# An attention block beside a gated MLP on one core: a third VectorE buffer, q masks and head packing by few DMAs over DRAM, the last softmax sums on TensorE, and new DMA times in the schedule model

## The chip, the core and the metric

The kernel runs on one core of a Trainium2 chip (trn2). A time is device microseconds of one execution. Each comparison below was run in rounds on one chip, the kernel beside the kernel before, and ratios are computed from these rounds: the mean time of one kernel's fast runs over the mean of the other's fast runs of the same rounds, so a ratio is not quite that of the medians that I quote. An interval is the 95% interval of that ratio. Profiles are of single executions, and single executions of one program differ here by about 1%.

## The reference

```python
xn = layernorm(x)                         # x: 1 x 2048 x 512, bf16
qkv = xn @ wqkv                           # H = 32 heads of Dh = 16
scores = einsum("bhqd,bhkd->bhqk", q, k) * 16 ** -0.5
o = einsum("bhqk,bhkd->bhqd", softmax(scores), v)
gate, up = xn @ W_gate, xn @ W_up         # 512 -> 1792
return x + o @ wo + (relu(gate) * up) @ W_down
```

32 heads times 2048 x 2048 scores are 134 million exponentials. They are the bulk of the work outside TensorE.

## The kernel before

ScalarE takes about 80% of the exponentials from PSUM (659 instructions on 1024 or 1536 columns). VectorE makes the other 20% (100 groups of four tiles) from bit arithmetic in five steps per group. TensorE makes the scores, the weighted sums of v ("PV"), the projections and the MLP, which are slotted in between. A score matmul sums over 32 rows, which hold two heads of 16, so q must be masked: `qm[:, slot, ee]` holds the rows of every second head and zeros elsewhere. ScalarE writes its exponentials into a ring of NRING buffers ("slots"), VectorE writes its own into NDR buffers; PV reads both, and a slot or buffer can be written again only when PV has read it.

The order of all instructions on all engines is fixed when the kernel is built. A small list scheduler in the kernel places each operation by an assumed duration and latency; on the chip every engine then executes its list in order, with semaphores. If an operation takes longer than the scheduler believed, whatever was placed behind it waits. The parts that the change touches:

```python
NRING = 7; PV_LAG = 7.0; PV_MIN = 0; NDR = 2     # NDR: VectorE's buffers
D_GROUPS = 100; D_SKIP = 10; D_TAIL = 12; D_LEAD = 11.0; D_WAIT = 6.0
RIDE = 40.0

def dma(fn, kb, ...):                            # the scheduler's idea of a DMA
    return G.op("SP", 120 + 3 * kb, fn, ..., lat=1900 + 2 * kb, ...)

def proj_q(c4, gg, ...):                         # q tile -> masked q
    G.op("DVE", 610, lambda e: e.tensor_copy(qT[:, tr.slot, :], bank_of(t, sub)), ...)
    for ee in range(2):
        for j in range(4):
            r0 = 32 * j + DH * ee
            dma(lambda e: e.dma_start(qm[r0:r0 + DH, tq.slot, ee, :], qT[r0:r0 + DH, tr.slot, :]), 16, ...)

def normalise(c4, gg, ee):                       # divide by the softmax sums
    G.op("DVE", 610, lambda e: e.tensor_copy(o_sb[...], ps_b[:, 0, :]), ...)
    dma(... rsum[:, par, :], o_sb[DH:128:32, to.slot, :] ..., 8)       # gather the sums
    G.op("DVE", 260, lambda e: e.reciprocal(rrec[...], rsum[...]), prio=-940)
    dma(... rec_scr[n] <- rrec ..., 8)                                 # to DRAM
    dma(... rb[...] <- rec_scr[n] broadcast to 32 rows each ..., 256)  # and back, spread
    G.op("POOL", 1200, lambda e: e.tensor_tensor(oT_of(tn), o_sb[...], rb[...], ALU.mult), ...)
    # [cut] the second of a pair of heads is packed beside the first by four DMAs of 16 KB
```

The softmax here doesn't subtract the row's maximum and nothing guards it: scores larger than these inputs give would overflow.

Of the kernel before, what the change touches and what calls it, by code (L numbers as in the profile page):

```python
# [5 lines left out]
BF16 = mybir.dt.bfloat16  # L6
# [22 lines left out]
NRING = 7  # L29
PV_LAG = 7.0  # L30
PV_MIN = 0
NWS = 3
NQ = 3
NDR = 2
KD = (1, 5, 9, 13)
D_GROUPS = 100
D_SKIP = 10
D_TAIL = 12
D_LEAD = 11.0
D_WAIT = 6.0  # L40
# [20 lines left out]
class Tile:  # L61
    def __init__(self, name="", pool=None, allowed=None):
        self.name = name
        self.pool = pool
        self.allowed = allowed
        self.slot = None
        self.w = []
        self.r = []


class Op:
    __slots__ = ("eng", "dur", "fn", "deps", "order", "prio", "acq", "name", "idx", "start", "end",
                 "done", "left", "users", "signal", "sem", "val", "waits", "stream", "lat", "seq", "hb", "after", "mode", "rows", "opens")


class Graph:
# [6 lines left out]
    RIDE = 40.0  # L83
# [11 lines left out]
    def op(self, eng, dur, fn, reads=(), writes=(), prio=0.0, order=(), name="", stream=None, lat=None, after=None, mode=None, rows=()):  # L95
        o = Op()
        o.rows = frozenset(rows)
        o.opens = None
        o.mode = mode
        o.eng, o.dur, o.fn, o.prio, o.name = eng, dur, fn, prio, name  # L100
        o.lat = self.LAT[eng] if lat is None else lat
        o.stream = stream
        o.after = after
        o.deps = {}
        o.order = set(order)
        o.acq = []
        o.done = False
        o.idx = len(self.ops)
        for t in reads:
            for w in t.w:  # L110
                o.deps[w] = True
        for t in writes:
            if t.pool is not None and not t.w:
                o.acq.append(t)
            for w in t.w:
                if w.eng == eng and eng == "PE":
                    o.order.add(w)
                else:
                    o.deps[w] = True
            for r in t.r:  # L120
                if r.eng == eng and eng in ("PE", "ACT"):
                    o.order.add(r)
                else:
                    o.deps[r] = True
        for t in reads:
            t.r.append(o)
        for t in writes:
            t.w.append(o)
        o.deps.pop(o, None)
        o.order.discard(o)  # L130
        self.ops.append(o)
        return o

    def run(self):
# [49 lines left out]
        def place(at, e, o):  # L184
            for t in o.acq:
                if t.slot is not None:
                    continue
                i = slot_for(t)[1]
                c = t.pool.cur[i]
                if c is not None:  # L190
                    for u in c.w + c.r:
                        if u.eng == e and e in ("PE", "ACT"):
                            o.order.add(u)
                        else:
                            o.deps[u] = True
                t.slot = i
                t.pool.cur[i] = t
            o.start = at
            o.end = at + o.dur + o.lat
            o.done = True  # L200
            o.seq = len(self.queue[e])
            self.queue[e].append(o)
            free[e] = max(free[e], at + o.dur)
            if o in cand[e]:
                cand[e].remove(o)
            for u in o.users:
                u.left -= 1
                if u.left == 0:
                    cand[u.eng].append(u)
# [12 lines left out]
        def blanks(at, o):  # L222

            while self.open is not None:
# [5 lines left out]
                b = self.op("PE", self.BLANK, self.fill, mode="col", name="blank")  # L230
                b.users, b.left = [], 0
                b.order.update(self.open)
# [5 lines left out]
        self.nblank = 0  # L238
        total = len(ops)
        while n < total:  # L240
# [27 lines left out]
            if e == "PE" and o.opens is not None:  # L268
                self.open = o.opens or None
            n += 1  # L270
# [117 lines left out]
def bass_parallel_sum__mha_block__glu_gated_reglu__prompt_kernel(  # L388
# [12 lines left out]
    rec_scr = nc.dram_tensor("rec_scr", [32, 4, 512], FP32, kind="Internal")  # L401

    with ExitStack() as es:
# [25 lines left out]
        qT = sb("qT", [128, 2, 512], BF16)  # L429
# [10 lines left out]
        oT2 = sb("oT2", [128, 2, 512], BF16)  # L440
        zeros = sb("zeros", [128, 512], BF16)
# [10 lines left out]
        P_qr = Pool("qr", 2)  # L452
# [5 lines left out]
        P_oT = Pool("oT", 10)  # L458
# [23 lines left out]
        t_qz = [Tile() for _ in range(NQ)]  # L482
        for i in range(1, NQ):
            G.op("POOL", 1000, lambda e, i=i: e.memset(qm[:, i, :, :], 0.0), writes=[t_qz[i]], prio=-480)
# [6 lines left out]
        def dma(fn, kb, writes=(), reads=(), prio=0.0, stream=None, order=(), name="dma", after=None):  # L491
            return G.op("SP", 120 + 3 * kb, fn, reads=reads, writes=writes, prio=prio, stream=stream or ("o", len(G.ops)),
                        lat=1900 + 2 * kb, order=order, name=name, after=after)

        x_src = x2.rearrange("(m p) d -> p m d", p=128)
        t_x = [Tile("x", P_x) for _ in range(NB)]
# [110 lines left out]
        def bank_of(t, sub=0):  # L607
            return ps_sc[:, 3 * t.slot + sub, :] if t.pool is P_sc else ps_b[:, t.slot, :]
# [13 lines left out]

        def proj_q(c4, gg, prio=0.0, tile=None, sub=0, eng="DVE", slots=None):
# [5 lines left out]
            if eng == "ACT":  # L629
# [3 lines left out]
                         reads=[t, t_mask], writes=[t_q1], prio=prio - 0.5)  # L633
                o.deps[tq.w[0]] = True
                tq.r.append(o)
            else:
                tr = Tile("qr", P_qr)
                G.op("DVE", 610, lambda e: e.tensor_copy(qT[:, tr.slot, :], bank_of(t, sub)), reads=[t], writes=[tr], prio=prio)
                for ee in range(2):
                    for j in range(4):  # L640
                        r0 = 32 * j + DH * ee
                        dma(lambda e, ee=ee, r0=r0: e.dma_start(qm[r0:r0 + DH, tq.slot, ee, :], qT[r0:r0 + DH, tr.slot, :]), 16,  # L642
                            reads=[tr] + t_qz, writes=[tq], prio=prio - 60, stream=("q%d" % (4 * ee + j), (4 * c4 + gg) % 2))
                        o = G.ops[-1]
                        for w in tq.w[:-1]:
                            o.deps.pop(w, None)
                            o.order.discard(w)
                        if (ee or j) and tq in o.acq:
                            o.acq.remove(tq)
# [80 lines left out]
        def heat(e):  # L730
            ins = None
            for _ in range(14):
                ins = e.matmul(ps_b[:, 1, :], zeros[:, 0:128], zeros[:], start=True, stop=True)
            return ins
        G.op("PE", 6000, heat, reads=[t_zero], writes=[tw0], prio=-900)
# [139 lines left out]
        pv_tile, last_rec, where = {}, {}, {}  # L875

        def normalise(c4, gg, ee):
# [5 lines left out]
            pr = upos(c4, gg, ee, NT) + 1  # L883
            ts, trr, tsc, trb = Tile("rs"), Tile("rr"), Tile("sc"), Tile("rb", P_rb)
            par = n % 2
            if n >= 2:
                ts.r.extend(last_rec[n - 2][0].r)
                trr.r.extend(last_rec[n - 2][1].r)
            dma(lambda e: e.dma_start(rsum[:, par, :], o_sb[DH:128:32, to.slot, :]), 8, reads=[to], writes=[ts], prio=pr - 50, stream=("n1", n % 4))
            G.op("DVE", 260, lambda e: e.reciprocal(rrec[:, par, :], rsum[:, par, :]), reads=[ts], writes=[trr], prio=-940)  # L890
            dma(lambda e: e.dma_start(rec_scr[n].rearrange("j (i q) -> (j i) q", q=16), rrec[:, par, :]), 8,
                reads=[trr], writes=[tsc], prio=pr - 50, stream=("n2", n % 4))
            last_rec[n] = (ts, trr)
            dma(lambda e: e.dma_start(rb[:, trb.slot, :], rec_scr[n].unsqueeze(1).to_broadcast([4, 32, 512])), 256,
                reads=[tsc], writes=[trb], prio=pr - 50, stream=("n3", n % 4))
            tn = Tile("oT", P_oT)
            G.op("POOL", 1200, lambda e: e.tensor_tensor(oT_of(tn), o_sb[:, to.slot, :], rb[:, trb.slot, :], ALU.mult),  # L897
                 reads=[to, trb], writes=[tn], prio=pr)
            if (c4, gg) == (NB - 1, NGG - 1):
                t_oT[(c4, NGG + ee)] = tn  # L900
            elif ee == 0:
                t_oT[(c4, gg)] = tn
            else:
                tw = t_oT[(c4, gg)]
                first_w = list(tw.w)
                for j in range(4):
                    dma(lambda e, j=j: e.dma_start(oT_of(tw)[32 * j + DH:32 * j + 32, :], oT_of(tn)[32 * j:32 * j + DH, :]), 16,
                        reads=[tn], writes=[tw], prio=pr, stream=("c%d" % j, gg % 2))
                    o = G.ops[-1]
                    for w in tw.w[:-1]:  # L910
                        if w not in first_w:
                            o.deps.pop(w, None)
                            o.order.discard(w)

        def pv_group(key, kt, u):
# [12 lines left out]
            for k in range(3 if on else 1):  # L928
# [9 lines left out]
                if first and k == 0:  # L938
                    G.ops[-1].opens = [G.ops[-1]]
                if last and k == (2 if on else 0):  # L940
                    G.ops[-1].opens = []
# [89 lines left out]
        tz = Tile("fin", P_sc, [0])  # L1031
        tz2 = Tile("fin2", P_b, [1])
        for i in range(4):
            out_rows(3, i, [5], False, True, pr=NU + 10 + i, tile=tz if i < 3 else tz2, sub=i if i < 3 else 0)

        def blank(e):
            ins = None
            for j in range(4):
                ins = e.matmul(ps_b[32 * j:32 * j + VN, 0, :], zeros[:, 0:VN], zeros[:], start=False, stop=False, tile_position=(0, 32 * j))  # L1039
            return ins  # L1040
        G.fill = blank
# [30 lines left out]
```

## Time and profile before

| | |
|---|---|
| time, median (of its 4 runs in the rounds of the comparison) | 890.1 us |
| the profiled execution | 898.1 us, span 896.3 us |
| first exponential starts / last ends | 17.6 / 876.4 us |
| ScalarE idle between the two | 101 us |
| TensorE's gaps over 1 us between the two | 9, together 20.9 us |

The prediction shows the lines of this profile and how each is read. Two more, which the argument needs later, come from the view of waits (engine and line that waited, what ended the wait; us in total, times, longest):

```profile
ACT ring L1020 <- PE ps_b L933: 54.8, 40, 5.9
...
DVE rrec L890 <- DMA rsum<-Wv: 10.1, 6, 2.8
```

The first says that ScalarE, before 40 of its exponentials, sat idle until TensorE was through with a PV matmul (L933). It was not waiting for scores. In one of these waits (timeline):

```profile
417.65 0.39 PE L952 MATMUL ps_sc<-qm,kT 32*128 32x512 bf16 x3
...
419.49 0.61 PE L933 MATMUL ps_b<-ring,v_aug 128*17 128x512 bf16 x8
...
419.93 1.45 ACT L1020 ACTIVATE ring<-ps_sc 128x1536 bf16<-128x1536 f32 x1 [2.00 <-PE ps_b L933]
```

The three scores of that exponential were done at 418.04, and it started only at 419.93, on the PV of 419.49 (whose end the profile models). Matching every exponential with its scores in the trace gives 38 waits, 54.0 us together, before which the scores had been ready for 1.67 us (median). In kernel.py an exponential depends on a PV only through the ring slot that it writes, so this row is ScalarE waiting for a free slot.

The second row is VectorE held by the small DMA that gathers the softmax sums. Each row names the last event before the wait ended, so by itself it is a pointer and not a proof.

### The profile page before, as it was taken

The page shows a single profiled execution, that of the slowest core. Times are in us where ns is not written, and L with a number is a line of the kernel's source. Part 1 is how long each engine was busy: PE and PEld are TensorE (multiplying, and loading weights), DVE is VectorE, ACT ScalarE, POOL GpSimd, SP SyncE. Part 2 cuts the span into 40 slices and gives each one's busy share as a digit, 9 for nine tenths or more (in the row PEclk, how much of TensorE's full clock was granted, in tenths as well). Part 3 has the DMA queues.
Part 4 walks back from the last instruction along what each step waited for, and adds up shares of the span by engine and source line. Part 5 has one row for each costly group of instructions (what it writes and reads, how often), then busy time and mean ns, then how long its engine had stood idle before and what let it go on. Part 6 is the DMA issues. An engine that isn't in the chain of part 4 may idle for free.

```text
span 896.3 us, 22022 instructions
## 1 busy us (share of the span) xinstructions
PE 823.7 (92%) x9722; PEld 239.2 (27%) x9722; DVE 774.7 (86%) x1116; ACT 762.2 (85%) x666; POOL 58.3 (7%) x58
## 2 busy tenths in 40 slices
PE   7999999999989989999989999999899999998992
PEld 3322222222222222222223222222222322222320
DVE  7999999899968979998896999998797989997842
ACT  4899989898969989899777999998797989985770
POOL 4100000100000000000000000000000000000000
PEclk8999999999999999999999999999899989998996
DMA  5023112111011111122010121112000121121001
GB/s 170 20 72 92 45 31 52 31 34 33 8 34 31 48 48 38 27 52 55 20 28 20 43 61 28 46 49 58 26 19 23 37 58 37 46 73 37 23 20 36
DMA packets 90031, 38.32 MB, mean 43 GB/s; under 512 B 72848, under 2 KB 85840, under 8 KB 89936
## 3 DMA queue, kind: packets, MB, share of 16 engines
q1 hardware_dynamic: 89936, 36.92, 15.8%
q8 instruction: 76, 1.25, 0.6%
q14 instruction: 19, 0.16, 0.1%
HBM read 31.33 MB, written 2.36 MB: 38 GB/s over the span
## 4 chain that ended last, share of the span: by engine, by line
PE 42%; DVE 38%; ACT 9%; DMA 5%; SPq 4%; issue 2%; POOLq 0%; POOL 0%
PE ps_b L617 15%; DVE dring L968 12%; PE ps_sc L952 10%; ACT ring L1020 9%; PE ps_b L933 9%; DVE dring L984 7%; DVE dring L985 5%; PE ps_b L952 4%; DVE dring L980 4%; SPq L642 3%; DVE dring L982 3%; PE ps_b L1039 3%; DVE up_sb L779 2%; DVE hT L783 2%; DVE Wv L882 1%
## 5 line engine op out<-in xcount | busy, mean ns | idle before, releaser
L1020 ACT ACTIVATE ring<-ps_sc 128x1536 bf16<-128x1536 f32 (+1 forms) x659 | 757.7, 1260 | 103.8 <-PE ps_b L933 54.8
L968 DVE TENSOR_SCALAR dring<-ps_b 128x512 uint16<-128x512 f32 x400 | 273.8, 685 | 40.5 <-PE ps_b L952 33.6
L952 PE MATMUL ps_sc<-qm,kT 32*128 32x512 bf16 x1648 | 267.3, 390 | 12.0 <-ACT ring L1020 5.0
L952 PE MATMUL ps_b<-qm,kT 32*128 32x512 bf16 x400 | 155.4, 388 | 15.5 <-DVE dring L968 13.4
L933 PE MATMUL ps_b<-ring,v_aug 128*17 128x512 bf16 x1648 | 141.0, 385 | 4.2 <-DVE Wv L882 4.2
L985 DVE TENSOR_TENSOR dring<-dring 128x2048 bf16<-128x2048 bf16 x100 | 126.6, 1266 | 0.2
L984 DVE TENSOR_TENSOR dring<-dring 128x2048 f16<-128x2048 bf16 x100 | 123.9, 1239 | 0.0
L952 PEld LDWEIGHTS ps_sc<-qm,kT 32*128 32x128 bf16 x1648 | 62.9, 91 | 227.0 <-ACT ring L1020 180.0
L1039 PE MATMUL ps_b<-zeros 128*17 128x512 bf16 x1020 | 84.0, 391 | 0.0
L897 POOL TENSOR_TENSOR x_sb<-Wv,rb 128x512 bf16<-128x512 f32 x26 | 37.9, 1458 | 665.0 <-DMA rb<-rec_scr 551.5
L617 PE MATMUL ps_b<-Wd,hT 128*32 128x512 bf16 x896 | 69.6, 403 | 7.5 <-DMA x_sb<-x_sb 7.5
L980 DVE TENSOR_SCALAR dring<-dring 128x2048 uint16<-128x2048 uint16 x100 | 70.5, 705 | 2.1
L933 PE MATMUL ps_b<-dring,vd 128*17 128x512 bf16 x800 | 70.8, 386 | 0.0
L617 PE MATMUL ps_b<-xnT,wgs 128*32 128x512 bf16 x896 | 66.8, 392 | 3.6 <-DVE up_sb L779 3.2
L982 DVE TENSOR_SCALAR dring<-dring 128x2048 uint16<-128x2048 uint16 x100 | 68.4, 684 | 0.0
L617 PE MATMUL ps_b<-xnT,wus 128*32 128x512 bf16 x896 | 67.7, 392 | 0.7 <-DVE hT L783 0.4
L952 PEld LDWEIGHTS ps_b<-qm,kT 32*128 32x128 bf16 x400 | 36.4, 91 | 99.2 <-DVE dring L968 67.7
L933 PEld LDWEIGHTS ps_b<-ring,v_aug 128*17 128x17 bf16 x1648 | 35.7, 89 | 64.3 <-issue 38.3
L933 PE MATMUL ps_b<-dring,v_aug 128*17 128x512 bf16 x400 | 39.8, 388 | 6.5 <-DVE dring L985 3.7
L783 DVE SCALAR_TENSOR_TENSOR hT<-ps_b,up_sb 128x512 bf16<-128x512 f32 x56 | 38.2, 683 | 8.3 <-PE ps_b L617 8.3
L779 DVE COPY up_sb<-ps_b 128x512 f32<-128x512 f32 x56 | 38.2, 683 | 7.6 <-PE ps_b L617 7.5
L1039 PEld LDWEIGHTS ps_b<-zeros 128*17 128x17 bf16 x1020 | 19.8, 89 | 38.1 <-issue 33.0
(67 smaller groups left out, 341.6 us busy)
## 6 DMA issues: line engine op xcount, KB each, us to landing
rb<-rec_scr SPq DMA_DIRECT2D x32, 256.0 KB
wus<-in_B_W_up_dram SPq DMA_DIRECT2D x56, 128.0 KB, 2.4
wgs<-in_B_W_gate_dram SPq DMA_DIRECT2D x56, 128.0 KB, 2.3
xr_sb<-in_A_x_dram SPq DMA_DIRECT2D x16, 128.0 KB, 4.0
out_dram<-xn_sb SPq DMA_DIRECT2D x16, 128.0 KB, 1.7
qm<-qT SPq DMA_DIRECT2D x120, 16.0 KB, 1.8
Wd<-in_B_W_down_dram SPq DMA_DIRECT2D x1, 1792.0 KB, 7.8
x_sb<-in_A_x_dram SPq DMA_DIRECT2D x3, 512.0 KB, 4.5
```

The source lines that it names most:

```text
L617: ins = e.matmul(bank_of(tile, sub)[32 * j:32 * j + 32, :], st[:, 32 * j:32 * j + 32], mv, start=(i == 0), stop=(i == n - 1), tile_positio ...
L779: G.op("DVE", 610, lambda e: e.tensor_copy(up_sb[:, tup.slot, :], bank_of(tu)), reads=[tu], writes=[tup], prio=slots[1])
L783: G.op("DVE", 610, lambda e: e.scalar_tensor_tensor(out=hT[:, FT * th.slot + ft, :], in0=bank_of(tg), scalar=0.0, in1=up_sb[:, tup.slot, : ...
L933: ins = e.matmul(ps_b[32 * j:32 * j + VN, 0, :], v, src[j][1](k), start=(first and k == 0), stop=(last and (k == 2 or not on)), tile_posit ...
L952: return e.matmul(bank, kT[32 * j:32 * j + 32, gg, 128 * kt:128 * kt + 128], qm[32 * j:32 * j + 32, t_q[(c4, gg)].slot, ee, :], start=True ...
L968: o = G.op("DVE", 610, lambda e, j=j: e.tensor_scalar(dring[:, tr.slot, 0, 512 * j:512 * j + 512].bitcast(U16), ps_b[:, 2, :], 0.25 * LOG2 ...
L980: G.op("DVE", 600, lambda e: e.tensor_scalar(b(2, U16), b(0, U16), 0x7F, 0x3F80, op0=ALU.bitwise_and, op1=ALU.bitwise_or), reads=[tr], wri ...
L982: G.op("DVE", 600, lambda e: e.tensor_scalar(b(1, U16), b(0, U16), 0xFF80, N_MANT, op0=ALU.bitwise_and, op1=ALU.bitwise_or), reads=[tr], w ...
L984: G.op("DVE", 1140, lambda e: e.tensor_tensor(b(2, FP16), b(2), b(2), ALU.mult), reads=[tm], writes=[tm], prio=u - 3, name="d4")
L985: G.op("DVE", 1140, lambda e: e.tensor_tensor(b(2), b(0), b(2, FP16), ALU.mult), reads=[tm, tr], writes=[tm], prio=u - 3, name="d5")
L1020: return e.activation(ring[:, a:a + n, :], ps_sc[:, 3 * k0:3 * k0 + n, :], ACTF.Exp, scale=0.25)
L1039: ins = e.matmul(ps_b[32 * j:32 * j + VN, 0, :], zeros[:, 0:VN], zeros[:], start=False, stop=False, tile_position=(0, 32 * j))
```

## The change

The intent is to let VectorE run further ahead (third buffer), to issue fewer DMAs, to make the scheduler believe more realistic DMA times, to take the DMAs out of the last normalisation, and to keep TensorE warm at the start and the end by "blanks", matmuls on zeros. The diff, cut to its core (cut too: qT and oT2 keep one buffer in place of two, other buffers shrink, and one mask operation of the start is placed later):

```diff
-NRING = 7
-PV_LAG = 7.0
-PV_MIN = 0
+NRING = 6
+PV_LAG = 4.0
+PV_MIN = 3
-NDR = 2
+NDR = 3
-D_GROUPS = 100
-D_SKIP = 10
-D_TAIL = 12
-D_LEAD = 11.0
-D_WAIT = 6.0
+D_GROUPS = 98
+D_SKIP = 14
+D_TAIL = 4
+D_LEAD = 10.0
+D_WAIT = 0.0
-    RIDE = 40.0
+    RIDE = 150.0
@@ the scheduler's DMA
+            if o.kb:
+                self.dq = max(self.dq, at + o.dur) + o.kb / 0.17
+                o.end = max(o.end, self.dq + 1500.0)
-            return G.op("SP", 120 + 3 * kb, fn, ..., lat=1900 + 2 * kb, ...)
+            o = G.op("SP", dur, fn, ..., lat=2000 if lat is None else lat, ...)   # dur=370 unless given
@@ proj_q: eight DMAs of 16 KB become a write and two reads of 128 KB
+                dma(lambda e: e.dma_start(q_scr[par, :, 0:DH, :], qT[:, tr.slot, :]), 128, ..., dur=500, lat=1400)
                 for ee in range(2):
-                    for j in range(4):
-                        r0 = 32 * j + DH * ee
-                        dma(lambda e, ee=ee, r0=r0: e.dma_start(qm[r0:r0 + DH, tq.slot, ee, :], qT[r0:r0 + DH, tr.slot, :]), 16, ...)
+                    dma(lambda e, ee=ee: e.dma_start(qm[:, tq.slot, ee, :], q_pick(par, ee)), 128, ..., dur=500, lat=1700)
+            # q_pick: ap=[(64 * 512, 4), (512, 32), (1, 512)]: rows of every second head, zeros between
@@ normalise: the packing likewise by a write for each head and one read for both
+            dma(lambda e: e.dma_start(o_scr[par, :, ee, :, :], oT_of(tn)), 128, ..., dur=500, lat=1400)
+                dma(lambda e: e.dma_start(oT_of(tw), src), 128, ..., dur=500, lat=1800)
@@ the last one
+            if (c4, gg, ee) == (NB - 1, NGG - 1, 1):
+                t_oT[(c4, NGG + ee)] = last_normalise(to, pr)   # fp32 matmuls, reciprocal, fp32 matmuls, multiply
+                return
@@ the last four output rows: a bank each instead of one tile for three
@@ heat_op.opens = ("start", [heat_op]): blanks also in the first microseconds
```

## The prediction

> **What bounds the kernel now.** I read the page's busy shares and slices first, then busy times by stretch, the waits, and the timeline around the longest stops.
>
> Busy shares, from the page (engine, busy us, share, instructions):
> ```profile
> span 896.3 us, 22022 instructions
> PE 823.7 (92%) x9722; PEld 239.2 (27%) x9722; DVE 774.7 (86%) x1116; ACT 762.2 (85%) x666; POOL 58.3 (7%) x58
> ```
> No engine is full. TensorE's 92% contains 84.0 us of "blank" matmuls on zeros (the row L1039 of the groups), which only keep it warm; without them TensorE, VectorE and ScalarE carry about the same work. The first exponential starts at 17.60 us and the last ends at about 876.4. In that stretch of 858 us ScalarE works 757 us, so it idles 101 us although it has a next exponential to do all the time. The whole question is what these 101 us, the head of 17.6 us and the tail of 20 us consist of.
>
> Busy times by stretch (start:end, length, then busy us of each engine, clock, DMA share, GB/s):
> ```profile
> 550.00:600.00 50.00, 47.37 (x566) 13.69 (x566) 48.31 (x69) 48.76 (x44) 2.84 (x2) 1.00 0.17 42
> 250.00:300.00 50.00, 46.25 (x565) 13.69 (x566) 38.71 (x54) 40.00 (x35) 1.93 (x2) 0.97 0.10 29
> 450.00:500.00 50.00, 45.83 (x553) 13.48 (x553) 39.31 (x56) 38.18 (x35) 2.55 (x2) 0.93 0.11 30
> ```
> In a good stretch VectorE and ScalarE reach 97% each. In a bad one both lose some 10 us out of 50, together: something stops all three. The timeline shows it twice, at 463 us and at 806 us. Of the second, some lines (start, length, engine, line, operation, in brackets the idle time before and what ended it; SPq is the queue that issues DMAs):
> ```profile
> 805.32 0.69 DVE L638 CAST qT<-ps_b 128x512 bf16<-128x512 f32 x1 [0.52 <-PE ps_b L617]
> ...
> 806.44 5.33 SPq L642 DMA_DIRECT2D qm<-qT  x8
> ...
> 813.09 0.61 PE L952 MATMUL ps_sc<-qm,kT 32*128 32x512 bf16 x3 [4.04 <-DMA qm<-qT]
> ...
> 813.74 2.37 ACT L1020 ACTIVATE ring<-ps_sc 128x1536 bf16<-128x1536 f32 x2 [7.85 <-PE ps_b L952]
> ```
> Eight small DMAs for one q mask take 5.33 us to issue, one after the other, and the last lands 1.8 us later: 7.0 us from the end of the cast (806.01) to the first score. The kernel's order comes from its own schedule model, which gives a DMA of 16 KB 120+3*16 = 168 ns of queue time and 1932 ns to landing, so 8*0.168+1.93 = 3.3 us. The static order was therefore laid 3.7 us too tight, and every engine is in order. At 252.8 and 467.1 us the same happens to the head packing: TensorE waits 2.78 and 2.83 us for x_sb<-x_sb, whose four issues stood behind the q DMAs.
>
> The tail, from the chain that ended last (start, length, what):
> ```profile
> 878.15 0.61 DVE Wv L882
> ...
> 878.78 1.84 DMA rsum<-Wv
> ...
> 880.64 0.26 DVE rrec L890
> ...
> 880.92 1.40 DMA rec_scr<-rrec
> ...
> 882.33 4.65 DMA rb<-rec_scr
> ...
> 887.08 1.30 POOLq L366
> ...
> 888.42 0.61 PE ps_sc L617
> ```
> From the copy's end at 878.76 to the output matmul at 888.42 are 9.66 us with nothing beside them.
>
> **What the Trainium skill says.** (1) "DMA: Bandwidth & Descriptors", section Rules for kernel authors: coalesce many small transfers, since below 64 KB one pays mostly overhead. The trace agrees: 16 KB land in 1.8 us, the 128 KB loads of wus in 2.4 us, and an issue costs 0.59 us for 16 KB as against 0.37 to 0.58 us for 128 KB. (2) "Perfetto Trace Analysis", section What "DMA-bound" means: one form is an issuing sequencer solid with DMA slices while little data moves. That is SPq at 806 us, with the DMA engines 16% busy in 800-850. (3) "TensorE: Matmul & The Clock Gate", section HAM oscillation: idle gaps of TensorE halve its clock. Here, after the gap of 4.04 us, the matmuls take 0.61 us where they took 0.39 before. (4) "FP8 and Floating Point Precision", section TensorE Precision Notes: true FP32 takes four passes. No run yet shows it; it concerns the new tail.
>
> **The change, part by part.**
>
> *Tail.* The new path has four fp32 matmuls that transpose the sums, a reciprocal of 128x16 (0.25 us, as L890), sixteen small fp32 matmuls that spread it, and a VectorE multiply (0.69 us). The transposes in bf16 took 0.22 us each; with four passes I estimate about 1.0 us for the four in fp32, and 1.2 us for the sixteen, four of which run side by side. With five handovers of 0.06 us the sum is 0.25+1.0+1.2+0.69+0.3 = 3.4 us in place of 9.66: 6.2 us less. Then the four last output rows: now three share one tile, so each matmul waits for the add before it (889.84, 891.26: 1.41 us apart). With a bank each the adds follow every 0.61 us, so that the last ends some 1.0 us earlier. Together **-7 us**.
>
> *Head.* The q and k projections at 12.3 to 15.9 us run cold (0.63 us a matmul, 1.9 us for sixteen, warm about 1.05). Warm blanks and a later mask op on VectorE should save up to 1.8 us; the PE is only lightly loaded there, so I take **-1.5 us**.
>
> *q masks and packing.* Per q tile 8 issues become 3, per pair of heads 4 become 3. That is 15*5+15*1 = 90 issues of some 0.59 us, 53 us of queue time, less. The latency is not shorter by much: estimated from the loads and stores in the trace, 0.5+1.7 for the write to DRAM, two issues of 0.5, then 2.4 for the second read's landing, so about 5.5 us instead of 7.0; for packing about 5 instead of 4.3. What changes is that the model now holds 4.6 us for q (0.5+1.4+0.5+0.5+1.7), so it errs by about 1 us and not by 3.7. ScalarE's idle time in the stretches 250-300, 450-500, 600-650, 650-700 and 800-850 is 10.0, 11.8, 9.7, 5.9 and 14.1 us; less 1 us each, as in a good stretch, these are 46 us. I take 55% of it as recovered: **-25 us**.
>
> *Third VectorE buffer, balance, new lags.* The other excess of ScalarE's idle time is 101-17-46 = 38 us (17 us being 1 us for each 50). The waits give VectorE 33.6 us for its single score bank and TensorE's weight loads 67.7 us for VectorE on that bank. A third buffer frees the order but adds no score bank. More of the 400 VectorE scores (230 of them run alone by their start times in the trace, at some 0.3 us each) may ride beside ScalarE's, as the model lets them ride up to 150 ns late instead of 40. I take a quarter: **-9 us**. Two groups fewer on VectorE take 2*(4*0.685+0.705+0.684+1.239+1.266) = 13.3 us off VectorE and put 8*0.427 = 3.4 us on ScalarE: **+2 us** on the end. One ring slot less and the DRAM round trips may cost new stops: **+5 us**.
>
> The sum is -7-1.5-25-9+2+5 = -35.5 us. From 889.0 that gives 853.5; I lean a little to the careful side and say **855 us**.
>
> **The rivals.** *The stop only moves.* The DRAM round trip has a write and a dependent read in series, and its reads have only four outer rows, like rb<-rec_scr, whose 256 KB take 4.65 us. If a 128 KB read took 3 to 4 us, the q path would again be 7 us and the stops stay; then only tail and head count, and the time is about 880. For it speaks rb's 4.65 us; against it that the model's figures for the other normalising DMAs (2.2, 1.44 and 5.1 us) are close to the trace's 1.84, 1.40 and 4.65, so the new figures look measured. *The three balanced engines hold it.* With VectorE and ScalarE both at 757 us of 858, removing one stop exposes the next: VectorE's wait for the single score bank. Then a third of the 46 us comes back and none of the 38: about 870. *Everything fits.* If all stretches reached the 97% of 550-600, the middle would take 757/0.97 = 780 us and the whole about 780+16+13+9 = 818, with 9 for what lies around; I think that is out of reach, but 840 is not.
>
> **Range and chances.** Tail and head together, 8.5 us, are nearly sure, but are under 1%. The 2% line is at 871.2 us and needs 17.8 us, so 9 us from the middle, a fifth of the stops that I can name. The range 838 to 874 runs from nearly all DMA stops gone to the second rival. Chances: faster 0.85, same 0.13, slower 0.02.
>
> **What would show it.** Right: no wait of TensorE over 2 us for a q or packing DMA; bad stretches near 45 us or more of ScalarE; ScalarE's idle time between first and last exponential near 65 us; from the last copy to the output matmul 3 to 4 us; SPq with 90 issues fewer; VectorE's 98 groups at the same 1.2 us a multiply. Wrong: if new gaps of TensorE of 3 us and more appear that end with a DMA from DRAM, the first rival holds; if no DMA gap is left and ScalarE still idles 90 us in pieces under 1 us, the second does. A clock under 0.95 in the middle would also break it.

## The result, and the profile after

The changed kernel takes 855.8 us (median of 4, 849.5 to 856.6) against 890.1 us: ratio 0.9599, interval 0.9556 to 0.9642. That is 34 us, and 855 was predicted. The profiled execution after is the fastest of its runs (849.5 us), and that of before (898.1 us) was slower than its median, so the two profiles differ by 48.6 us of span; some 14 us of that belong to the executions and not to the change.

The page after (as before: engine, busy us, share, instructions):

```profile
span 847.7 us, 21183 instructions
PE 785.1 (93%) x9378; PEld 227.3 (27%) x9378; DVE 759.2 (90%) x1101; ACT 765.6 (90%) x670; POOL 56.9 (7%) x58
```

The work is nearly the same; the span is shorter because VectorE and ScalarE are idle less. The stretches that were good and bad before (the same times do not hold quite the same work in both kernels):

```profile
250.00:300.00 50.00, 48.00 (x621) 14.12 (x610) 43.53 (x60) 48.05 (x43) 3.90 (x2) 1.00 0.16 49
...
450.00:500.00 50.00, 49.44 (x630) 14.48 (x626) 43.37 (x60) 49.46 (x44) 2.71 (x2) 1.00 0.19 52
...
550.00:600.00 50.00, 46.40 (x554) 13.37 (x554) 48.20 (x69) 47.55 (x42) 2.54 (x2) 1.00 0.24 62
```

ScalarE went from 40.0 and 38.2 us in the bad stretches to 48.1 and 49.5. So far this looks like the prediction come true. The waits after say otherwise:

```profile
ACT ring L1086 <- PE ps_b L1018: 24.3, 19, 4.5
...
ACT ring L1086 <- PE ps_b L999: 5.0, 3, 4.2
...
DVE rrec L956 <- DMA rsum<-Wv: 18.8, 8, 3.3
```

What vanished is ScalarE's wait for PV matmuls (now L999): 54.8 us became 5.0. What grew are its waits that end with a score of VectorE (L1018 into ps_b; 14.5 us before) and a wait for a DMA: 10.1 us became 18.8. And TensorE still has 10 gaps over 1 us between the first and the last exponential, together 23.1 us against 20.9. The DMA stops did not go away. One of them in the timeline after (L674 writes q to DRAM, L677 are the two reads, L955 gathers the sums of another head):

```profile
706.11 0.61 SPq L674 DMA_DIRECT2D q_scr<-qT  x1
708.96 1.15 SPq L677 DMA_DIRECT2D qm<-q_scr  x2
710.15 0.57 SPq L955 DMA_DIRECT2D rsum<-Wv  x1
714.56 0.25 DVE L956 RECIPROCAL rrec<-rsum 128x16 f32<-128x16 f32 x1 [3.19 <-DMA rsum<-Wv]
...
715.42 1.35 PE L643 MATMUL ps_b<-xnT,wgs 128*32 128x512 bf16 x16 [3.17 <-DVE up_sb L812]
...
717.36 1.45 ACT L1086 ACTIVATE ring<-ps_sc 128x1536 bf16<-128x1536 f32 x1 [3.44 <-PE ps_sc L1018]
```

The gathering of 8 KB was issued at 710.15 right behind the reads of 2 x 128 KB and let VectorE go on only at 714.56, after 4.4 us; its median over the run is 1.87 us. It is no single case: the seven gatherings that were issued within 5 us after a q read took 3.8 to 5.2 us to land, the other 24 at most 2.2 us, and none took over 2.1 us within 5 us after a small q DMA in the kernel before. VectorE's list stood still at the reciprocal, then TensorE for lack of an evacuated bank, then ScalarE.

How long do the DMAs over DRAM take? From issue to the last update of the semaphore in the trace: the q write 2.6 us, the first q read 4.1, the second 4.9, the packing write 3.3 and its read 3.3 (medians); the loads of wgs, also 128 KB, 2.3 us. The eight small q DMAs before took 6.8 us from the first issue to the last landing (median of the 15 q tiles), the write and two reads take 8.2. The semaphores point to a reason: a load of wgs makes 16 updates, so does a small q DMA of 16 KB, a q write makes 9, a q read 5. The Trainium skill, "DMA: Bandwidth & Descriptors", section Why a DMA increments its semaphore by 16 and not by 1, says that such a DMA runs on the k DMA engines, at most 16, that divide the slowest dimension of both access patterns, each posting one update, and the issuer the rest at once. The pattern of `q_pick` starts with a 4: four engines and the issuer's one are the 5 updates seen, and the write with its 8 blocks gives 9. The trace agrees with the page. The gathering of the sums also makes 5 updates, so by the same rule it has four engines; that it queued on the very four that the q reads used fits its 4.4 us, but the trace as I read it does not name the engine of a packet, so this stays an inference. Nor did any run change the number of engines alone, so that the reads are slow because they have four is argued and not shown.

The tail after, from the chain that ended last:

```profile
837.78 0.66 DVE Wv L945
...
838.48 1.05 PE ps_b L920 x8
...
839.88 1.12 PE ps_sc L930 x32
841.03 0.70 DVE x_sb L936
...
841.78 0.83 PE ps_sc L643 x12
```

From the copy's end (838.44) to the output matmul are 3.3 us in place of 9.66.

### The profile page after: what moved, and what is told of

The parts are those of the page before. It is cut to its first block, busy times and chain, and to the rows that moved or that the text cites. A ratio compares the mean times of both kernels' runs of the same rounds, so it can differ in the third digit from the quotient of the medians.

```text
span 847.7 us, 21183 instructions
## 1 busy us (share of the span) xinstructions
PE 785.1 (93%) x9378; PEld 227.3 (27%) x9378; DVE 759.2 (90%) x1101; ACT 765.6 (90%) x670; POOL 56.9 (7%) x58
## 4 chain that ended last, share of the span: by engine, by line
DVE 50%; PE 34%; DMA 9%; ACT 4%; issue 1%; SPq 1%; POOL 0%; DVEq 0%; POOLq 0%
DVE dring L1034 16%; PE ps_b L643 14%; PE ps_sc L1018 9%; DVE dring L1050 8%; DVE dring L1051 8%; PE ps_b L999 7%; DVE dring L1046 4%; ACT ring L1086 4%; DVE dring L1048 4%; DMA rsum<-Wv 4%; DVE up_sb L812 3%; PE ps_b L1018 2%; DVE hT L816 2%; DVE Wv L945 1%; DMA q_scr<-qT 1%; DMA qm<-q_scr 1%
## 5 line engine op out<-in xcount | busy, mean ns | idle before, releaser
L1034 DVE TENSOR_SCALAR dring<-ps_b 128x512 uint16<-128x512 f32 x392 | 267.8, 683 | 40.1 <-PE ps_b L1018 36.4
L1018 PE MATMUL ps_sc<-qm,kT 32*128 32x512 bf16 x1656 | 272.9, 392 | 3.8 <-ACT ring L1086 1.9
L1018 PE MATMUL ps_b<-qm,kT 32*128 32x512 bf16 x392 | 153.8, 392 | 24.0 <-DVE dring L1034 16.9
L999 PE MATMUL ps_b<-ring,v_aug 128*17 128x512 bf16 x1656 | 155.6, 389 | 2.4 <-DVE Wv L945 2.3
L1018 PEld LDWEIGHTS ps_sc<-qm,kT 32*128 32x128 bf16 x1656 | 63.5, 91 | 230.8 <-ACT ring L1086 171.5
L1051 DVE TENSOR_TENSOR dring<-dring 128x2048 bf16<-128x2048 bf16 x98 | 121.4, 1239 | 0.1
L1050 DVE TENSOR_TENSOR dring<-dring 128x2048 f16<-128x2048 bf16 x98 | 120.5, 1229 | 0.0
L1046 DVE TENSOR_SCALAR dring<-dring 128x2048 uint16<-128x2048 uint16 x98 | 70.8, 722 | 1.5
L1048 DVE TENSOR_SCALAR dring<-dring 128x2048 uint16<-128x2048 uint16 x98 | 71.3, 727 | 0.0
L999 PE MATMUL ps_b<-dring,vd 128*17 128x512 bf16 x784 | 69.5, 390 | 0.0
L1018 PEld LDWEIGHTS ps_b<-qm,kT 32*128 32x128 bf16 x392 | 35.7, 91 | 89.9 <-DVE dring L1034 61.7
L999 PEld LDWEIGHTS ps_b<-ring,v_aug 128*17 128x17 bf16 x1656 | 38.3, 89 | 73.9 <-issue 56.3
L1116 PE MATMUL ps_b<-zeros 128*17 128x512 bf16 x624 | 54.5, 397 | 0.0
L999 PE MATMUL ps_b<-dring,v_aug 128*17 128x512 bf16 x392 | 39.5, 393 | 4.0 <-DVE dring L1051 3.7
L816 DVE SCALAR_TENSOR_TENSOR hT<-ps_b,up_sb 128x512 bf16<-128x512 f32 x56 | 38.2, 682 | 0.8 <-PE ps_b L643 0.7
L643 PEld LDWEIGHTS ps_b<-xnT,wgs 128*32 128x32 bf16 x896 | 18.3, 95 | 37.4 <-DVE up_sb L812 17.0
```

What stands on the lines that cost most here:

```text
L643: ins = e.matmul(bank_of(tile, sub)[32 * j:32 * j + 32, :], st[:, 32 * j:32 * j + 32], mv, start=(i == 0), stop=(i == n - 1), tile_positio ...
L816: G.op("DVE", 610, lambda e: e.scalar_tensor_tensor(out=hT[:, FT * th.slot + ft, :], in0=bank_of(tg), scalar=0.0, in1=up_sb[:, tup.slot, : ...
L999: ins = e.matmul(ps_b[32 * j:32 * j + VN, 0, :], v, src[j][1](k), start=(first and k == 0), stop=(last and (k == 2 or not on)), tile_posit ...
L1018: return e.matmul(bank, kT[32 * j:32 * j + 32, gg, 128 * kt:128 * kt + 128], qm[32 * j:32 * j + 32, t_q[(c4, gg)].slot, ee, :], start=True ...
L1034: o = G.op("DVE", 610, lambda e, j=j: e.tensor_scalar(dring[:, tr.slot, 0, 512 * j:512 * j + 512].bitcast(U16), ps_b[:, 2, :], 0.25 * LOG2 ...
L1046: G.op("DVE", 600, lambda e: e.tensor_scalar(b(2, U16), b(0, U16), 0x7F, 0x3F80, op0=ALU.bitwise_and, op1=ALU.bitwise_or), reads=[tr], wri ...
```

## The experiments

Twelve kernels ran, eleven of them the changed kernel with a part undone or altered, and all were correct. Where I convert a ratio into us, 1% is 8.9 us.

**1. All the schedule parameters back** (`a_oldparams`).

```diff
-NRING = 6; PV_LAG = 4.0; PV_MIN = 3; NDR = 3; D_GROUPS = 98; D_SKIP = 14; D_TAIL = 4; D_LEAD = 10.0; D_WAIT = 0.0; RIDE = 150.0
+NRING = 7; PV_LAG = 7.0; PV_MIN = 0; NDR = 2; D_GROUPS = 100; D_SKIP = 10; D_TAIL = 12; D_LEAD = 11.0; D_WAIT = 6.0; RIDE = 40.0
```

> The changed kernel with all the schedule parameters of the kernel before (two VectorE buffers, seven ring slots, PV_LAG 7, PV_MIN 0, 100 VectorE groups, skip 10, tail 12, lead 11, wait 6, ride 40). New DMAs, new tail and new head stay. Theory 1, as predicted: the stops came from the DMAs and their model, so the middle keeps most of its gain: at most 864 us. Theory 2: the third buffer and the new lags made the middle shorter: 872 to 880 us, that is only tail and head gained.

Measured: 894.1 us, ratio 1.0023 (0.9987 to 1.0059): as slow as the kernel before, although it has the new DMAs, the new tail and the new head. Theory 1, mine, falls: without the new parameters the DMA part gains nothing. Even theory 2 was too kind to it, since tail and head had shortened and the time had not. In its waits:

```profile
ACT ring L1086 <- PE ps_b L999: 47.1, 36, 4.4
```

**2. The third buffer alone taken away** (`a_ndr2`).

```diff
-NDR = 3
+NDR = 2
```

> The changed kernel with two VectorE buffers in place of three, nothing else. Theory 1 (DMAs): within 4 us of the changed kernel, 852 to 860 us. Theory 2 (third buffer): 866 us or more.

Measured: 884.9 us, ratio 0.9928 (0.9882 to 0.9974). Against the changed kernel's 0.9599 that is 3.3%, some 29 us, for one buffer of VectorE. Theory 2 holds. The same wait for ring slots is back in part:

```profile
ACT ring L1086 <- PE ps_b L999: 29.7, 23, 4.8
```

The buffer joins all three engines. The PVs of one head stand in TensorE's list in a fixed order, those of VectorE's groups among them. With two buffers a group of VectorE can only begin after TensorE has read an older one in PV, so its own PV comes late in the list, the PVs behind it come late too, and with them the ring slots that they free for ScalarE. The wait is 54.8, 47.1, 46.2 (experiment 4) and 29.7 us with two buffers, 5.0 with three and 11.5 in experiment 3. Three buffers do not forbid it: experiment 12 has 59.3 us of it, by another order. The third buffer was taken away here from a kernel whose lags and ring were set for three; adding it alone to the kernel before was not run.

**3. Eight small q DMAs again, with their measured times in the scheduler** (`a_q8`).

```diff
-  dma(q_scr <- qT, 128, dur=500, lat=1400); 2 x dma(qm <- q_pick, 128, dur=500, lat=1700)
+  8 x dma(qm[r0:r0+16, slot, ee] <- qT[r0:r0+16], 16, dur=590.0, lat=1240.0)
```

> The changed kernel with the q masks by eight small DMAs of 16 KB again, but with their measured times in the schedule model (0.59 us to issue each, 1.83 us to landing). Theory 1 (fewer DMAs matter): 862 us or more, as the queue is again held 5 us for each q tile. Rival: in the profile of the changed kernel the path over DRAM takes some 8.4 us (2.6 for the write, 4.9 for the second read), the eight small ones took 7.0 us, so with a true model they cost nothing or gain: 850 to 857 us.

Measured: 828.5 us, ratio 0.9278 (0.9231 to 0.9325). That is 3.2%, some 29 us, faster than the changed kernel and below everything that I had expected, the rival included. The round trip over DRAM, with the times that the scheduler held for it, was the costly part of the change; experiment 6 parts the two. TensorE's gaps over 1 us fell from 10 (23.1 us) to 5 (8.8 us), and

```profile
DVE rrec L947 <- DMA rsum<-Wv: 2.8, 5, 1.0
```

**4. The kernel before with nothing but measured DMA times in its scheduler** (`b_model`).

```diff
-  dma: SP 120 + 3 * kb, lat=1900 + 2 * kb
+  dma: SP 370, lat=2000 + 2 * kb; q and packing 590 + 1240 (1230); sums 600 + 1600; reciprocals 340 + 1100; broadcast 580 + 4500
```

> The kernel before with nothing but measured DMA times in its schedule model (q and packing 0.59 us each, sums 0.6+1.6, reciprocals 0.34+1.1, broadcast 0.58+4.5, loads 0.37). Theory 1 (the wrong DMA times in the model made the stops): 866 to 872 us, most of the 25 us of the prediction. Theory 2 (buffers and lags): within 5 us of the kernel before, 885 to 893 us.

Measured: 871.9 us, ratio 0.9773 (0.9718 to 0.9828): 20 us gained with the same buffers and the same DMAs. Here theory 1 is right: a scheduler that knows its DMAs removes their stops (TensorE's gaps over 1 us: 3, together 3.3 us, against 9 with 20.9). The PV wait is untouched, as it should be if it comes from the buffers:

```profile
ACT ring L1020 <- PE ps_b L933: 46.2, 36, 3.4
```

**5. A control: how much is chance?** (`a_jitter`)

```diff
-  LAT = {..., "DVE": 100.0, ...}
+  LAT = {..., "DVE": 105.0, ...}
```

> A control: the changed kernel with one latency of its schedule model changed from 100 to 105 ns (VectorE's), which lays the static order of TensorE and of the DMA queue anew without changing any part. If order by chance matters little, 850 to 861 us; if it lies outside, differences of that size between the other runs tell nothing.

Measured: 861.9 us, ratio 0.9655 (0.9595 to 0.9714). A latency changed by 5 ns gives another order of TensorE's list; the time came out 0.6%, some 5 us, longer, just outside what I had allowed, though the intervals overlap. So differences of under about 1% between kernels whose order was laid anew are not read as effects below. One draw does not bound what a new order can do (experiment 12 lost 40 us by one); more weight lies in effects that came back in a second order, as the third buffer's (experiments 2 and 11) and that of q (3, 7 and 8) did.

**6. The DRAM path with the times that it has** (`a_truelat`).

```diff
-  q write 500 + 1400, q reads 500 + 1700, packing write 500 + 1400, packing read 500 + 1800
+  q write 610 + 2010, q reads 545 + 3600 and 545 + 4350, packing write 550 + 2780, packing read 615 + 2650
```

> The changed kernel with the times that its own profile shows for the DMAs over DRAM put in the schedule model (q write 2.6 us, q reads 4.1 and 4.9 us, packing write 3.3 us, packing read 3.3 us); the program's parts are the same. Theory 1 (a path that the model holds for 3.8 us shorter than it is makes the stops, so knowing it is enough): 832 to 845 us. Theory 2 (the slow reads on four DMA engines do the harm themselves, by their length and by holding up the sums behind them): 850 to 860 us.

Measured: 845.0 us, ratio 0.9503 (0.9435 to 0.957), between the two ranges. It is 1.0% under the changed kernel, but the intervals overlap and it is no more than the control's size, so the part due to wrong times is by the means about a third of the 29 us (the intervals allow 1 to 16 us). It is still 2.3% above the eight small DMAs, which is well outside the control: knowing the path's length isn't enough. TensorE keeps 9 gaps over 1 us, together 16.5 us.

**7. The packing by four small DMAs too** (`a_q8_pack4`).

```diff
-  o_scr <- oT (128 KB) for each head, oT <- o_scr (128 KB) for both
+  4 x dma(oT[32j+16:32j+32] <- oT'[32j:32j+16], 16, dur=590.0, lat=1230.0)
```

> Eight small DMAs for q and four for the packing, as in the kernel before, with measured times in the model; all else as in the changed kernel. If the DRAM round trip of the packing (3.3+3.3 us against 4.2) costs as the one of q does: 818 to 826 us. If packing has slack (its readers come many units later): the same as with the eight q DMAs alone, 826 to 832 us.

Measured: 829.7 us, ratio 0.9296 (0.9229 to 0.9363), the same as with eight q DMAs alone. The packing has slack; the cost was in q.

**8. No DMA for q at all** (`a_qpool_pack4`, packing as in 7).

```diff
-  q_scr <- qT; qm <- q_pick (2x)
+  G.op("POOL", 1000, e.tensor_scalar(qm[:, slot, 0, :], qT, hmask[:, 0:1], None, op0=ALU.mult))
+  G.op("POOL", 1000, e.tensor_scalar(qm[:, slot, 1, :], qT, hmask[:, 1:2], None, op0=ALU.mult))
```

> The q masks made on chip by two multiplies on GpSimd, no DMA at all for q; packing by four small DMAs. If what matters is that q comes early and that the DMA queue is free: 815 to 828 us. If GpSimd's work hinders VectorE or the normalising on GpSimd: 830 us or more.

Measured: 822.8 us, ratio 0.9234 (0.9181 to 0.9288). It beats the kernel before by 7.7% and the changed kernel by 3.7%; over the eight small DMAs its lead is within the intervals. GpSimd was 93% idle after the change, and its two multiplies (1.77 and 1.90 us in the trace) take 3.7 us where the path over DRAM takes 8.2. The scheduler held them for 1.0 us each, so this kernel is fast without true times for q. ScalarE idles 33 us between its first and last exponential, against 62 in the profile of the changed kernel.

**9. The last sums by DMA again** (`a_tail_dma`). The order of all engines is the same but for the last instructions.

```diff
-            if (c4, gg, ee) == (NB - 1, NGG - 1, 1):
+            if False:
```

> The changed kernel with the last softmax sums by DMA again (only the last ten or so instructions differ; the four rows keep a bank each). In its profile the TensorE path takes 3.3 us from the copy's end to the output matmul, the DMA path of the kernel before 9.66. Theory: 6.3 us longer, 861 to 863 us. Rival: the end is set by something else too (out rows, other DMAs), then less than 3 us.

Measured: 861.6 us, ratio 0.9642 (0.9618 to 0.9666), 0.4% or some 4 us above the changed kernel by the ratios, 5.8 us by the medians. The chain has the DMAs back, and from the copy's end (844.05) to the output matmul are 9.65 us, 6.3 more than with TensorE:

```profile
844.07 1.82 DMA rsum<-Wv
...
846.20 1.40 DMA rec_scr<-rrec
...
847.61 4.64 DMA rb<-rec_scr
...
853.70 0.65 PE ps_sc L643 x4
```

So the mechanism and its size hold in the profile; the times agree within their intervals.

**10. No blanks at the start** (`a_head_cold`). Only TensorE's blanks differ.

```diff
-        heat_op.opens = ("start", [heat_op])
```

> The changed kernel without the blanks of the first microseconds; orders of all other engines stay the same. The first exponential came 3.6 us earlier than in the kernel before. Theory of the prediction (cold projections): 1 to 2 us longer, with the projections at 0.63 us a matmul. Rival: the whole 3.6 us is warmth, so 3 us or more longer. Second rival: the earlier layer norm gives it, and less than 1 us is lost.

Measured: 857.2 us (median of its five fast runs; a sixth was slow and is left out), ratio 0.9583 (0.9555 to 0.961), against 0.9599 with them: no difference. TensorE was cold indeed. The K projection in this run, then the first exponential (timeline):

```profile
11.00 1.93 PE L643 MATMUL ps_b<-xnT,Wk 128*32 128x512 bf16 x16
...
14.75 3.71 ACT L1086 ACTIVATE ring<-ps_sc 128x1536 bf16<-128x1536 f32 x3 [2.79 <-PE ps_sc L1018]
```

With blanks the same projection takes 1.03 us and the first exponential starts at 13.99, so warmth is worth 0.76 us. The head became 3.6 us shorter in all, and most of the rest comes from before the projections: their first matmul starts at 9.98 us after and at 12.31 us before, 2.3 us earlier. The second rival holds. In the profile of before a tiny VectorE operation (L469, 128x2) took 1.87 us beside a memset on GpSimd, and after, with another memset beside it, 0.20 us; whether that is the cause I did not test.

**11. Does the third buffer only bridge late q tiles?** (`a_q8_ndr2`)

```diff
 (a_q8)
-NDR = 3
+NDR = 2
```

> Eight small DMAs for q with measured times, and two VectorE buffers in place of three. With q over DRAM the third buffer was worth 29 us. If it is worth that by itself: 855 us or more. If it mostly bridged late q tiles: at most 842 us.

Measured: 859.4 us (median of its three fast runs), ratio 0.9637 (0.9593 to 0.9681), 3.6% or some 32 us slower than with three buffers. The buffer is worth the same with early q tiles as with late ones, so the two effects are separate.

**12. VectorE's and GpSimd's measured times in the scheduler too** (`a_best`).

```diff
 (a_qpool_pack4)
-  G.op("DVE", 610 | 600 | 1140, ...); G.op("POOL", 1280, ...)
+  G.op("DVE", 685 | 700 | 1235, ...); G.op("POOL", 1450, ...)
```

> Q masks on GpSimd, packing by four small DMAs, and VectorE's and GpSimd's times in the model as the traces show them (685, 700, 1235 and 1450 ns in place of 610, 600, 1140 and 1280). If a truer model makes a better order for VectorE as it did for the DMAs: 810 to 820 us; if not, 820 to 828 us.

Measured: 862.8 us, ratio 0.9664 (0.9636 to 0.9691): some 40 us slower than without it, a clear miss. The truer scheduler put in 318 groups of four blanks instead of 170, and ScalarE waits for ring slots again, with three buffers:

```profile
ACT ring L1068 <- PE ps_b L981: 59.3, 35, 4.4
```

The lags and the numbers of groups were chosen with the old VectorE times, and I did not choose them anew.

**What the scheduler planned.** The scheduler in a run's kernel.py can be run without the chip, with the instructions replaced by dummies; it then lays as many blanks as the trace shows. The end of its plan beside the measured median, and the exponentials whose ring slot is freed by a PV that stands behind their own score in TensorE's list:

| kernel | planned, us | measured, us | slot after score |
|---|---|---|---|
| before | 848 | 890 | 82 of 659 |
| `b_model` | 847 | 872 | 68 of 659 |
| changed | 795 | 856 | 6 of 663 |
| `a_ndr2` | 823 | 885 | 49 of 663 |
| `a_truelat` | 803 | 845 | 9 of 663 |
| `a_q8` | 801 | 829 | 13 of 663 |
| `a_q8_ndr2` | 825 | 859 | 45 of 663 |
| `a_best` | 860 | 863 | 82 of 663 |

The third buffer is worth 28 and 24 us in the plans alone (823 to 795, 825 to 801). The q path shows in how far the chip falls behind its plan: 61 us in the changed kernel, 42 with true times, 28 with eight small DMAs. And the 40 us that `a_best` lost are in its plan, which the chip then kept to within 3 us; why VectorE times longer by 8 to 17% lead the scheduler to so poor an order stays open.

## Why the prediction was right in its number, and where its reasons were wrong

The number was right to 1 us, but by luck: the sum was not made of the right terms.

| term | predicted | measured |
|---|---|---|
| tail | -7 us | TensorE path 3.3 us for 9.66: -6.3 in the profile; last sums by DMA again cost 4 to 6 us of time |
| head | -1.5 us | first exponential 3.6 us earlier; 0.76 of it from warm projections, no difference in time |
| q masks and packing with a better model | -25 us | about +7 us or more (what is left over, see below) |
| third buffer, lags, ring, balance | -9+2+5 = -2 us | -38 us, of which -29 the buffer |
| sum | -35.5 us | about -36; measured -34 |

How the measured terms come about: the kernel with old parameters (experiment 1) has all of the change but these, and is 2 us above the kernel before by its ratio. Less the tail's 4 to 6 us, that leaves some +7 for the DMA part, and more if the earlier start is worth something. The parameters are 1.0023 against 0.9599, 4.2%, or 38 us. The DMA term is thus found by subtraction, so that the measured terms add up is no check of them; experiments 3, 7 and 8, which replace the q path, are.

- *The stops come from a schedule that holds its DMAs for too short.* Right, and shown by experiment 4: measured times alone gave the kernel before 20 us, near the 25 predicted. But this is not what the change did. The step that failed is "the model now holds 4.6 us for q ... so it errs by about 1 us and not by 3.7". The path took 2.6 us for the write, 0.6 until the second read was issued and 4.9 for that read to land, 8.2 us in all (median), so the model erred by 3.6 us, as much as before.
- *The path is "about 5.5 us instead of 7.0".* Wrong, it became longer, 8.2 us against 6.8 from the first issue to the last landing. (The 7.0 starts at the end of the cast. "The last lands 1.8 us later" misreads the line: it is 1.8 us from the last DMA's own issue, some 1.3 after the eight are issued.) I took 2.4 us for a read from loads that run on sixteen DMA engines; these ran on four. My first rival named this ("only four outer rows, like rb<-rec_scr") and guessed 3 to 4 us; I turned it down because the new model's figures for other DMAs were close to the trace. They were, but those for q were not.
- *"A third buffer frees the order but adds no score bank."* This is the other step that failed. I looked at VectorE's waits for its score bank (33.6 us before, 36.4 us for the same row after: unchanged, as I said) and passed over the row with 54.8 us in which ScalarE waited for PV to free a ring slot. That row fell to 5.0 us with the third buffer.
- *Issues.* 180 small ones became 90, as worked out. It brought nothing that a run shows: the kernels with 120 q issues are the faster ones.
- *What should show it.* "No wait of TensorE over 2 us for a q or packing DMA" was wrong: TensorE waited 3.28 us for q at 773.9 and 2.99 us for a packed pair at 648.0. ScalarE's idle time "near 65 us" came out: 62 us in this profile, 65 and 74 in experiments 9 and 10, whose ScalarE order is the same. "3 to 4 us" in the tail was right. By my own text new gaps of 3 us and more that end with a DMA from DRAM mean that the first rival holds. There is one such gap, and the rival's mechanism holds by experiments 3, 7 and 8; its 880 us does not, because of a gain that none of the three stories had.

Two errors of over 30 us each, with opposite signs, cancelled. A right number is no proof of the reasons for it; only undoing each part was.

## What to carry to other kernels

Where every engine runs a fixed list, ask for each wait in the profile which engine's list it holds up, and count the wait at the engine that starves (here ScalarE for a ring slot) before the one whose buffer is changed. Look up in the program which dependency joins the two instructions that a wait names: it can be a buffer to be freed and not the data. Compare the time that the scheduler planned with the measured one: it parts a poor order from an order that the chip cannot keep. Fewer and larger DMAs are no gain in themselves: compare the whole path from issue to landing and the number of DMA engines that each pattern can use, and look for an idle engine that makes the copy unnecessary. When a change has several parts, undo each by itself, with a control for how much a mere reordering is worth.

## What the Trainium skill lacked or had wrong

- "DMA: Bandwidth & Descriptors", Rules for kernel authors: the advice to coalesce transfers below 64 KB would have one write and two reads of 128 KB in place of eight copies of 16 KB. Here the eight took 6.8 us and the three 8.2 us, and the kernel with the eight was 29 us faster. The condition that the large transfer keeps its sixteen engines stands in the same table, in another row (Use all 16 engines: a short outermost dimension confines the DMA to that many), to which the advice does not point; that a round trip adds a second landing is not said there.
- The same page gives the rule for the number k of engines, and the semaphore updates here (16, 9 and 5) agree, but it gives no times by k. For 128 KB these runs show 2.3 us with k = 16 (wgs from DRAM), 2.6 us with k = 8 (q to DRAM), 3.3 us with k = 8 (packing from DRAM), 3.3 us with k = 4 (packing to DRAM), and 4.1 and 4.9 us for two q reads with k = 4 issued together.
- The same page gives no figure for what a large DMA on few engines does to a small one behind it: 8 KB on four engines took 3.8 to 5.2 us in the seven cases behind two such reads, where its median is 1.87 us.
- "FP8 and Floating Point Precision", TensorE Precision Notes, counts four passes for true FP32. The trace lists two matmul instructions for each fp32 matmul (8 for 4, 32 for 16). The sixteen small ones took 1.08 us; what passes lie within an instruction, it does not show.
- No page speaks of an order of instructions fixed by assumed times: a change of 5 ns in an assumed latency gave a time 0.6% longer (the intervals overlap), and truer VectorE times made one kernel 40 us slower.
